# First loads on other queues, and unit 2's state half and block around the first feed-forward groups

## The chip, the cores and the metric

The kernel runs on one core of a Trainium2 chip. Its engines run side by side, each with its own queue of instructions, and wait for each other by semaphores: PE (TensorE, matmuls; its weight loads are listed as PEld), DVE (VectorE), ACT (ScalarE), POOL (GpSimd) and SP (SyncE, which here only starts transfers). SP, ACT and POOL can all start DMA transfers. The profile has one row for the transfers that POOL issues (software queue) and other rows for those of SP and ACT (hardware queues).

The metric is device time in microseconds (us), the median of several runs. The profile is that of one execution, and its times count from the first instruction.

## The reference: what is computed

A retention layer, and then a two-layer feed-forward network with a quick GELU.

```python
scores = scale * np.matmul(q, k.transpose(0, 1, 3, 2))      # q, k, v: 8 x 8 heads x 576 x 64
gamma = 1.0 - 2.0 ** (-5.0 - np.arange(H))
Dmat = np.where(rel >= 0, gamma[:, None, None] ** rel[None, :, :], 0.0)   # rel = i - j
ret = scores * Dmat[None, :, :, :]
x = np.matmul(ret, v)            # then tokens x (heads * 64): 4608 x 512
h = x @ w_in                     # 512 x 2048
g = h * (1.0 / (1.0 + np.exp(-1.702 * h)))
out = g @ w_out                  # 2048 x 512
```

Inputs and output are float32; the kernel's matmuls read bfloat16.

## The kernel before

**Units and chunks.** The 4608 tokens are cut into 36 units of 128 tokens, and four units make a chunk of 512. Since the decay gamma^(i-j) is a product of a factor of i and a factor of j, a unit needs no full score matrix: within each half of 64 tokens it uses masked scores, and what lies before comes from a running state (a sum of k times v over the earlier halves). V is multiplied by its factor on DVE (`scale_v`, L345, into `vp`) and the result by the factor of the query (`x_out`, L534, from PSUM times `gq` into `xT`).

**One unit of the beginning** (units 0 to 3) goes through these steps:

- `load(u)`: three transfers of 256 KB, K and Q (L226; units 1 and 2 load Q by L213) and V (L239). They are issued by POOL. K and Q are cast to bfloat16 on the way.
- `transpose_pe` (L361, L356): four or eight transposes on TensorE into PSUM, one set for K and one for Q, and `transpose_copy` on ACT (L374) or DVE (L377) into `kqT`.
- `scores(u)` (L497) on TensorE into psC and psD, `scores_out` (L506) on DVE: times the mask, into `pm`.
- `state_half(u, 0)`: `update`, eight matmuls k times vp into psK (L403), and a copy of psK on ACT into `kv` (L413).
- `block1(u)`: `inter` (L481, the state against Q), `values` (L519, pm against vp), in between `state_half(u, 1)`, and then the two `x_out` on DVE.

**Unit 0 is loaded apart.** `load_kq0` brings its K and its Q uncast into the output tiles osb1 and osb2, both issued by SP (L246), and `cast_kq0` casts them on DVE (L257). Its V comes as the first transfer on POOL's queue.

**The feed-forward part.** `up_group(c, f0, nf, lo, hi, bank)` multiplies nf of the 16 column blocks of w_in with the units lo to hi of chunk c (L570) and applies the GELU on ACT (L575); `up` is the same for a whole chunk (L556, GELU L561). `down` multiplies with w_out (L582), its result is copied (L592) and stored (L598). In the first chunk the up-groups are placed between the steps of the units as soon as x of two units is there.

**What sets the order.** The order of each engine's instructions is written out by hand in `lead_in` (units 0 to 7, chunk 0) and `steady` (the rest); the class `Program` finds the waits from the tiles that are read and written. Every engine takes its instructions strictly in that order. `lead_in` begins with the transfers: POOL makes three iotas and then issues V of unit 0, K, Q and V of units 1 and 2, two parts of w_in, unit 3, the rest of w_in, w_out, and units 4 to 11. `warm(n, bank, w)` puts n matmuls (L674) of w columns (512 if not told otherwise) on zeros in between; they give nothing that is used. ACT begins with the exponentials for the decay factors: eight `vfac` (L307), four `gq_first` (L315), four `g_powers` (L321), and then a small GELU (L687) that has the table of that function loaded early.

From unit 8 on K and Q are transposed by DMA, issued by SP (L391, `dma_transpose`). The first of these, unit 8, is placed after the load of V of unit 13, and the others of that group follow it in SP's queue:

```python
                    for u in range(8, 14):
                        dma_transpose(u, ["vn1"])
```

Here vn1 is the tile that holds V of unit 13 by then.

Of the kernel before, what the change touches and what calls it, by code (L numbers as in the profile page):

```python
# [11 lines left out]
B, H, S, DH = 8, 8, 576, 64  # L12
# [17 lines left out]
class Program:  # L30
# [10 lines left out]
    def op(self, eng, fn, reads=(), writes=(), dma=None, ndma=1, after_ops=()):  # L41
        o = Op()
        o.eng, o.fn, o.dma, o.signal, o.count = eng, fn, dma, False, None
        o.idx = len(self.streams[eng]) + 1
        deps = {}
        for k in reads:
            for d in self.writers.get(k, ()):
                deps[id(d)] = (d, True)
        for k in writes:
            for d in self.writers.get(k, ()) + self.readers.get(k, ()):  # L50
                deps.setdefault(id(d), (d, False))
        known = self.known[eng]
        need = []
        for d, raw in deps.values():
            if d.dma is None:
                if d.eng == eng and dma is None and (eng == "pe" or not raw):
                    continue
                agent, val = d.eng, d.idx
            else:
                agent, val = d.dma, d.dval  # L60
            need.append((agent, val, d))
        for d in after_ops:
            need.append((d.eng, d.idx, d))
        need.sort(key=lambda x: -x[1])
        waits = {}
        for agent, val, d in need:
            if known.get(agent, 0) >= val:
                continue
            if agent in waits and waits[agent][0] >= val:
                continue  # L70
            waits[agent] = (val, d)
        pruned = []
        for agent, (val, d) in waits.items():
            if any(
                a2 != agent and d2.known.get(agent, 0) >= val
                for a2, (_, d2) in waits.items()
            ):
                continue
            pruned.append(d)
        for agent, (val, d) in waits.items():  # L80
            d.signal = True
            known[agent] = max(known.get(agent, 0), val)
            for a2, v2 in d.known.items():
                if v2 > known.get(a2, 0):
                    known[a2] = v2
        o.waits = pruned
        o.known = dict(known)
        if dma is None:
            o.known[eng] = max(o.known.get(eng, 0), o.idx)
        else:  # L90
            self.dma_count[dma] = self.dma_count.get(dma, 0) + 16 * ndma
            o.dval = self.dma_count[dma]
            o.known[dma] = o.dval
        self.streams[eng].append(o)
        for k in writes:
            self.writers[k] = (o,)
            self.readers[k] = ()
        for k in reads:
            self.readers[k] = self.readers.get(k, ()) + (o,)
        return o  # L100
# [60 lines left out]
def bass_retnet_parallel__then__act_gelu_quick_kernel(  # L161
# [10 lines left out]
    with es:  # L172
# [35 lines left out]
        op = pr.op  # L208
# [25 lines left out]
        def load_v(u, after=(), eng="pool"):  # L234
            sl = u % NLD

            def f(e):
                return [
                    e.dma_start(vn[sl][p0 : p0 + n, :, :], v[b, :, s0 : s0 + n, :].rearrange("h p d -> p h d"))  # L239
                    for p0, n, b, s0 in unit_rows(u)  # L240
                ]
            op(eng, f, reads=after, writes=[f"vn{sl}"], dma=f"d_vn{sl}_{eng}", ndma=len(unit_rows(u)))

        def load_kq0(which):
            src = (k, q)[which]
            op("sp", lambda e: e.dma_start(  # L246
                osb[1 + which].ap().rearrange("p (h d) -> p h d", d=DH),
                src[0, :, 0:P, :].rearrange("h p d -> p h d")),
               writes=[f"osb{1 + which}_0"], dma=f"d_kq0f_{which}")
# [438 lines left out]
               reads=["warm"], writes=["gelu_table"])  # L688

        def lead_in():  # L690
            load_kq0(0)
            load_kq0(1)
            iota_small()
            iota_large()
            load_v(0)
            load(1)
            load(2)
            load_win(0, 2)
            load_win(2, 2)
            load(3)  # L700
            load_win(4, 2)
            load_win(6, 2)
            load_win(8, 4)
            load_win(12, 4)
            for i in range(4):
                load_wout(i)
            for u in range(4, NPE + 4):
                load(u)
            op("dve", lambda e: e.memset(gT[1][:, 0, :], 0.0), writes=["warm"])
            warm_quads(NQUAD)  # L710
            warm(44, "A", 64)
            setup_dve()
            setup_dve2()
            setup_vfac()
            for a in range(4):
                gq_first(a)
            g_powers()
            gelu_table()
            cast_kq0(0, "dve")
            transpose_pe(0, 0, "E")  # L720
            transpose_copy(0, 0, "E", "dve")
            cast_kq0(1, "dve")
            warm(4)
            transpose_pe(0, 1, "B")
            transpose_copy(0, 1, "B", "dve")
            scale_v(0)
            warm(2)
            scores(0)
            scores_out(0, 1, 0)
            scores_out(0, 1, 1)  # L730
            warm(1, "A", 256)
            state_half(0, 0)
            transpose_pe(1, 0, "E")
            transpose_copy(1, 0, "E", "act")
            transpose_pe(1, 1, "B")
            transpose_copy(1, 1, "B", "act")
            scale_v(1)
            block1(0)
            warm(1, "A", 256)
            scores(1)  # L740
            scores_out(1, 1, 0)
            scores_out(1, 1, 1)
            gq_next(1)
            warm(1)
            state_half(1, 0)
            transpose_pe(2, 0, "E")
            transpose_copy(2, 0, "E", "act")
            warm(1)
            block1(1)
            transpose_pe(2, 1, "B")  # L750
            transpose_copy(2, 1, "B", "act")
            warm(2)
            scores(2)
            scale_v(2)
            scores_out(2, 1, 0)
            scores_out(2, 1, 1)
            up_group(0, 0, 2, 0, 2, "A")
            state_half(2, 0)
            up_group(0, 2, 2, 0, 2, "B")
            gq_next(2)  # L760
            block1(2)
            transpose_pe(3, 0, "E")
            transpose_copy(3, 0, "E", "dve")
            transpose_pe(3, 1, "D")
            transpose_copy(3, 1, "D", "act")
            up_group(0, 0, 4, 2, 3, "A")
            scale_v(3)
            scores(3)
            scores_out(3, 1, 0)
            scores_out(3, 1, 1)  # L770
            gq_next(3)
            warm(1, "E", 256)
            state_half(3, 0)
            up_group(0, 4, 2, 0, 2, "B")
            block1(3)
            up_group(0, 4, 2, 2, 3, "A")
            up_group(0, 6, 2, 0, 2, "B")
            up_group(0, 0, 4, 3, 4, "C")
            up_group(0, 4, 2, 3, 4, "A")
            up_group(0, 6, 2, 2, 4, "B")  # L780
            gq_next(4)
            gq_next(5)
            for f in range(8, NF):
                up(0, f)
            def ahead45():
                ahead(2)
                for u in (4, 5):
                    state_sum(u, 0)
                    state_sum(u, 1)
                state_cast(4, 6)  # L790
                scores_out(4, 2, 0)
                scores_out(4, 2, 1)

            work = {
                (1, 3): lambda: (scale_v(4), transposes(4, "E", "D", "dve")),
                (2, 0): lambda: (transposes(5, "E", "D", "dve"), scale_v(5)),
                (2, 1): ahead45,
                (3, 1): lambda: block(2, lambda: None),
                (3, 2): lambda: (transposes(6, "C", "D", "dve"), scale_v(6)),
                (3, 3): lambda: (transposes(7, "E", "K", "dve"), scale_v(7)),  # L800
            }
            for r, s in [(i % 2, i // 2) for i in range(8)] + [(i // 4, i % 4) for i in range(8, NF)]:
                down(0, r, s, "AB"[r % 2])
                if (r, s) in work:
                    work[r, s]()
                if s == 3:
                    finish_unit(0, r, "AB"[r % 2])
# [130 lines left out]
```

## Time and profile before

| what | value |
| --- | --- |
| median of the runs | 295.63 us (295.49, 295.63, 296.52) |
| span of the profiled execution | 293.4 us |
| what lies around the span, against the median | 2.2 us |
| TensorE busy | 287.7 us, 98% |
| ScalarE, GpSimd, VectorE busy | 133.7, 110.2, 99.7 us |
| moved by DMA | 40.63 MB, mean 139 GB/s |
| share of POOL's queue, of SP's (of 16 engines' span) | 68.0%, 24.8% |
| mean granted TensorE clock | 0.999 |

The profile lists for an instruction its start, its duration, its engine and line, and what it writes and reads (out<-in, numbers of tiles left out). In brackets stands the time for which the engine had been idle and what ended that. For a DMA the duration is that of issuing it; the time to landing is told apart. The chain of waits goes back from the last instruction to whatever released it. The profiled execution's time outside the span is not recorded; it is taken as the difference to the median of the runs.

In the first microseconds the transfers land as follows, from the start of their issue (from the rows of the single lines): K of unit 0 after 3.1 us, Q of unit 0 after 3.5, V of unit 0 after 6.5, K, Q and V of unit 1 after 5.7, 5.4 and 5.5. DMA engines moved 279 GB/s from 2.2 to 4.4 us, 178 and 186 in the two microseconds after that, and 204 from 20 to 24 us.

### The profile page before, as it was taken

To read this page: it belongs to the slowest core of one execution; us is meant where nothing else is said; L and a number is where in the kernel's file an instruction comes from. 1 tells how busy PE (TensorE), PEld (TensorE's weight loads), DVE (VectorE), ACT (ScalarE), POOL (GpSimd) and SP (SyncE) were. 2 spreads that over 40 slices of the span, in tenths; PEclk is the share of its full clock that TensorE was granted. 3 is DMA by queue.
4 is the path that set the end of the run, shared out by engine and by line. 5 is a ranking of instruction groups with operands and counts; after the bars stand their busy time and mean duration, and the time that the engine had idled before them with its cause. 6 is when DMAs were issued, how large, how long until landed. Compare 5 with 4: busy or idle time off the path is not lost.

```text
span 293.4 us, 8059 instructions
## 1 busy us (share of the span) xinstructions
PE 287.7 (98%) x3650; PEld 141.2 (48%) x3650; DVE 99.7 (34%) x202; ACT 133.7 (46%) x235; POOL 110.2 (38%) x141
## 2 busy tenths in 40 slices
PE   8899999999999999999999999999999999999996
PEld 6575456775533553345334533454344434443344
DVE  5861056615650652054404360237013700410000
ACT  7466234661366135712672256324642365216611
POOL 9999798000960590292049103910170000000000
PEclk9999999999999999999999999999999999999999
DMA  9999999998999899799479935992692050111022
GB/s 172 175 211 206 209 231 249 235 120 213 125 236 115 98 230 227 93 161 200 133 106 153 188 108 113 178 182 80 137 142 71 20 131 2 38 72 38 0 65 78
DMA packets 116786, 40.63 MB, mean 139 GB/s; under 512 B 104080, under 2 KB 109968, under 8 KB 116752
## 3 DMA queue, kind: packets, MB, share of 16 engines
q0 software_dynamic: 79712, 22.82, 68.0%
q1 hardware_dynamic: 36896, 17.24, 24.8%
q8 instruction: 28, 0.46, 0.7%
q10 hardware_dynamic: 144, 0.07, 0.1%
q14 instruction: 6, 0.05, 0.0%
HBM read 36.70 MB, written 9.44 MB: 157 GB/s over the span
## 4 chain that ended last, share of the span: by engine, by line
PE 96%; DMA 2%; DVE 1%; issue 0%; ACT 0%; POOL 0%; POOLq 0%
PE psA L582 22%; PE psB L582 21%; PE psA L556 18%; PE psB L556 18%; PE psB L570 4%; PE psA L570 3%; DMA vn<-in_v_dram 2%; PE psX L481 2%; PE psC L497 1%; PE psY L519 1%; PE psX L519 1%; PE psK L426 1%; PE psD L497 1%; PE psE L426 1%; PE psK L403 1%; PE psE L361 0%
## 5 line engine op out<-in xcount | busy, mean ns | idle before, releaser
L226 POOL DMA_DIRECT2D kqn<-in_k_dram x39 | 35.1, 910 | 106.9 <-DMA kqT<-kqn 104.9
L582 PE MATMUL psA<-w_out_sb,gT 128*128 128x512 bf16 (+1 forms) x304 | 69.4, 371 | 0.3 <-issue 0.3
L582 PE MATMUL psB<-w_out_sb,gT 128*128 128x512 bf16 (+1 forms) x288 | 65.4, 376 | 0.0
L556 PE MATMUL psA<-xT,w_in_sb 128*128 128x512 bf16 x240 | 61.6, 379 | 0.0
L556 PE MATMUL psB<-xT,w_in_sb 128*128 128x512 bf16 x240 | 61.6, 379 | 0.0
L544 DVE TENSOR_TENSOR xT<-psX,gq 128x512 bf16<-128x512 f32 x16 | 11.1, 691 | 109.3 <-PE psX L519 109.3
L450 ACT ACTIVATE kv<-stm 128x1024 bf16<-128x1024 f32 (+1 forms) x18 | 15.6, 866 | 68.7 <-DVE stm L441 68.7
L582 PEld LDWEIGHTS psB<-w_out_sb,gT 128*128 128x128 bf16 x288 | 27.8, 98 | 32.5 <-ACT gT L561 0.3
L561 ACT ACTIVATE gT<-psB 128x512 bf16<-128x512 f32 x60 | 35.8, 597 | 15.8 <-PE psB L556 15.7
L561 ACT ACTIVATE gT<-psA 128x512 bf16<-128x512 f32 x60 | 35.8, 597 | 15.6 <-PE psA L556 15.6
L582 PEld LDWEIGHTS psA<-w_out_sb,gT 128*128 128x128 bf16 x304 | 27.2, 98 | 31.9 <-ACT gT L561 2.5
L239 POOL DMA_DIRECT2D vn<-in_v_dram x40 | 37.1, 942 | 0.1
L556 PEld LDWEIGHTS psA<-xT,w_in_sb 128*128 128x128 bf16 x240 | 19.2, 97 | 32.7 <-ACT gT L561 16.6
L556 PEld LDWEIGHTS psB<-xT,w_in_sb 128*128 128x128 bf16 x240 | 18.8, 97 | 33.0 <-ACT gT L561 16.4
L345 DVE TENSOR_TENSOR vp<-vn,vfac 128x512 bf16<-128x512 f32 x36 | 23.4, 684 | 30.8 <-DMA vn<-in_v_dram 30.8
L226 POOL DMA_DIRECT2D kqn<-in_q_dram x37 | 33.4, 917 | 0.6 <-issue 0.6
L592 ACT ACTIVATE osb<-psB 128x512 f32<-128x512 f32 (+1 forms) x18 | 10.6, 590 | 22.7 <-PE psB L582 22.5
L592 ACT ACTIVATE osb<-psA 128x512 f32<-128x512 f32 x18 | 10.5, 584 | 15.3 <-PE psA L582 15.3
L506 DVE TENSOR_TENSOR pm<-psC,mask 128x512 bf16<-128x512 f32 (+1 forms) x20 | 12.6, 628 | 8.7 <-PE psD L497 8.7
L506 DVE TENSOR_TENSOR pm<-psD,mask 128x512 bf16<-128x512 f32 (+1 forms) x20 | 12.5, 626 | 0.0
L570 PE MATMUL psB<-xT,w_in_sb 128*128 128x256 bf16 x96 | 12.5, 273 | 0.0
L441 DVE TENSOR_TENSOR stm<-psE,stm 128x256 f32<-128x256 f32 x28 | 11.9, 424 | 1.2
(86 smaller groups left out, 257.3 us busy)
## 6 DMA issues: line engine op xcount, KB each, us to landing
vn<-in_v_dram POOLq DMA_DIRECT2D x32, 256.0 KB, 5.6
out_dram<-osb SPq DMA_DIRECT2D x31, 256.0 KB, 2.6
kqn<-in_k_dram POOLq DMA_DIRECT2D x31, 128.0 KB, 5.5
kqn<-in_q_dram POOLq DMA_DIRECT2D x31, 128.0 KB, 5.7
w_out_sb<-in_moe_w_out_dram POOLq DMA_DIRECT2D x4, 512.0 KB, 13.3
w_in_sb<-in_moe_w_in_dram POOLq DMA_DIRECT2D x8, 128.0 KB, 5.0
w_in_sb<-in_moe_w_in_dram POOLq DMA_DIRECT2D x4, 256.0 KB, 7.2
vn<-in_v_dram POOLq DMA_DIRECT2D x8, 128.0 KB, 7.0
```

The lines of the kernel that those rows point to most:

```text
L226: e.dma_start(kqn[sl][p0 : p0 + n, which, :, :], src[b, :, s0 : s0 + n, :].rearrange("h p d -> p h d"),)
L239: e.dma_start(vn[sl][p0 : p0 + n, :, :], v[b, :, s0 : s0 + n, :].rearrange("h p d -> p h d"))
L345: op(eng, lambda e: e.tensor_tensor(vp[u % NVP].ap(), vn[sl].ap(), vfac[:, ty, :, None].to_broadcast([P, H, DH]), ALU.mult), reads=[f"vn{s ...
L441: op("dve", lambda e: e.tensor_tensor(dst, src, prev, ALU.add), reads=[KB[a], f"stm{(i - 1) % 8}"], writes=[f"stm{i % 8}"])
L450: op("act", lambda e: e.activation(kv[:, i0 % NKV : i0 % NKV + n, :, :], stm[:, i0 % 8 : i0 % 8 + n, :, :], AF.Copy), reads=[f"stm{(i0 + i ...
L506: op("dve", lambda e: e.tensor_tensor(pm[(u0 // 2) % 2][hh][:, c0:c1].rearrange("p (a i) -> p a i", i=64), ps32(SB[hh])[:, c0:c1].rearrang ...
L544: op("dve", lambda e: e.tensor_tensor(xT[ch % 2][:, slice(hh, 4, 2), P * jj : P * jj + 2 * P].rearrange("p g (u t) -> p u g t", u=2), ps32 ...
L556: op("pe", lambda e, a=a: e.matmul(bank[b][:, n0:n1], w_in_sb[:, a, P * f : P * f + P], xT[c % 2][:, a, n0:n1], start=(a == 0), stop=(a == ...
L561: op("act", lambda e: e.activation(gT[c % 2][:, f, n0:n1], bank[b][:, n0:n1], AF.Gelu_apprx_sigmoid), reads=[b], writes=[f"g{c % 2}_{f}_{j ...
L570: op("pe", lambda e, a=a, f=f, i=i: e.matmul(bank[b][:, n * i : n * i + n], w_in_sb[:, a, P * f : P * f + P], xT[c % 2][:, a, P * lo : P * ...
L582: op("pe", lambda e, f=f: e.matmul(bank[b][:, 0 : n1 - n0], gT[c % 2][:, f, P * r : P * r + P], w_out_sb[:, f, n0:n1], start=(f == 0), sto ...
L592: op("act", lambda e: e.activation(dst, src, AF.Copy), reads=[b], writes=[f"osb{i}_{n0}"])
```

## The change

Four edits in `lead_in`, and a parameter for `load_kq0`:

- K of unit 0 stays on SP; Q of unit 0 is issued by ACT, as its first instruction; V of unit 0 is issued by SP, behind K, and is no longer on POOL's queue.
- The cast of Q of unit 0 goes from DVE to ACT, between the second and the third of the four `gq_first`.
- Warming matmuls: one instead of four ahead of Q's transposes, three of 512 columns instead of one of 256 ahead of unit 0's first state half, and none instead of one of 256 ahead of unit 3's.
- `state_half(2, 0)` stands ahead of the first feed-forward group instead of behind it, and `gq_next(2)` and `block1(2)` stand ahead of the second group instead of behind it.

```diff
-        def load_kq0(which):
+        def load_kq0(which, eng):
             src = (k, q)[which]
-            op("sp", lambda e: e.dma_start(
+            op(eng, lambda e: e.dma_start(
...
         def lead_in():
-            load_kq0(0)
-            load_kq0(1)
+            load_kq0(0, "sp")
+            load_kq0(1, "act")
+            load_v(0, eng="sp")
             iota_small()
             iota_large()
-            load_v(0)
             load(1)
...
             setup_vfac()
-            for a in range(4):
-                gq_first(a)
+            gq_first(0)
+            gq_first(1)
+            cast_kq0(1, "act")
+            gq_first(2)
+            gq_first(3)
             g_powers()
             gelu_table()
             cast_kq0(0, "dve")
             transpose_pe(0, 0, "E")
             transpose_copy(0, 0, "E", "dve")
-            cast_kq0(1, "dve")
-            warm(4)
+            warm(1)
             transpose_pe(0, 1, "B")
...
             scores_out(0, 1, 1)
-            warm(1, "A", 256)
+            warm(3)
             state_half(0, 0)
...
             scores_out(2, 1, 1)
+            state_half(2, 0)
             up_group(0, 0, 2, 0, 2, "A")
-            state_half(2, 0)
-            up_group(0, 2, 2, 0, 2, "B")
             gq_next(2)
             block1(2)
+            up_group(0, 2, 2, 0, 2, "B")
             transpose_pe(3, 0, "E")
...
             gq_next(3)
-            warm(1, "E", 256)
             state_half(3, 0)
```

## The prediction

> **What bounds the kernel now.** I read the page's share of busy time first, then the chain of waits over the first 40 us, then the order of time of the first 10 us, and last the landings of single transfers.
>
> ```profile
> span 293.4 us, 8059 instructions
> PE 287.7 (98%) x3650; PEld 141.2 (48%) x3650; DVE 99.7 (34%) x202; ACT 133.7 (46%) x235; POOL 110.2 (38%) x141
> ```
>
> TensorE is 98% busy and is the chain that ended last for 96% of the span. From 24.7 us on its matmuls follow one another, so nothing there is for this change to win; all it can do is let the dense part start earlier. A microsecond won in the first 25 us is worth a microsecond at the end, if no transfer is late afterwards. The chain (start, us, what) shows what the start waits for:
>
> ```profile
> 1.42 6.49 DMA vn<-in_v_dram
> ...
> 16.83 0.77 DVE xT L534 x2
> ...
> 18.95 0.21 PE psE L674
> ```
>
> The first V (unit 0) is issued by POOL at 1.42 and lands at 7.91; only then can DVE scale it and TensorE make the first state half, at 8.68. At 16.83 TensorE waits for the two x_out products of unit 2, although two transposes lie beside them; the groups after it start at 17.64. The last line is a warming matmul that computes nothing. In the order of time (start, us, engine, line, tile; in brackets the idle time before it):
>
> ```profile
> 0.73 0.46 SPq L246 DMA_DIRECT2D osb<-in_k_dram  x1
> 1.25 0.57 SPq L246 DMA_DIRECT2D osb<-in_q_dram  x1
> ...
> 1.42 1.03 POOL L239 DMA_DIRECT2D vn<-in_v_dram  x1
> ...
> 3.46 1.63 ACT L315 ACTIVATE gq<-iota_c,lnsc,lng 128x128 f32<-128x128 f32 x4
> ...
> 4.87 1.69 PE L674 MATMUL psA<-gT 128*128 128x512 bf16 x4
> ...
> 5.46 0.60 DVE L257 CAST kqn<-osb 128x512 bf16<-128x512 f32 x1
> ...
> 6.62 0.59 PE L674 MATMUL psA<-gT 128*128 128x512 bf16 x2
> ...
> 7.93 0.69 DVE L345 TENSOR_TENSOR vp<-vn,vfac 128x512 bf16<-128x512 f32 x1 [0.69 <-DMA vn<-in_v_dram]
> ...
> 9.54 0.69 DVE L345 TENSOR_TENSOR vp<-vn,vfac 128x512 bf16<-128x512 f32 x1 [0.26 <-DMA vn<-in_v_dram]
> ```
>
> Four warming matmuls at 4.87 take 1.69 us, two at 6.62 take 0.59: the array runs at half speed until about 6.2 us. The last two rows say that V is late twice: unit 0 by 0.69, unit 1 by 0.26. Unit 1's transfers stand right behind the first V on POOL's queue.
>
> One place far from the change matters as well. SyncE's transpose of unit 9 starts at 64.8 and lands 2.7 later, at 67.55; TensorE reads it for unit 9's scores at 67.60. SyncE's queue had waited for V of unit 13, which POOL issued at 50.1 and which landed 12.6 later (the waits of SyncE's queue; us in total, times, longest):
>
> ```profile
> SPq L116 <- DMA vn<-in_v_dram: 12.3, 1, 12.3
> ```
>
> So at 67.6 us TensorE and the stream of transfers meet within 0.05 us. TensorE can be earlier there only by as much as POOL's stream is earlier.
>
> **The change part by part.** Times are in the profiled execution, whose span is 293.4; the median of the runs shown, 295.63, lies 2.2 above it, which is what stands around a span and is left as it is.
>
> *K, Q and V of unit 0.* K keeps its place on SP (0.73). Q's issue (0.57) moves to ScalarE, ahead of its first table load (1.28 from 0.73). That load then ends near 2.6; the first exponential waited until 2.67 for DVE anyway, so the issue costs nothing; without that cover it would cost its 0.57. V takes Q's place on SP at 1.25. K alone needed 3.06 from issue to landing, Q behind it 3.55. K now shares the engines with Q: it lands between 3.80 (as now) and 4.80 (when both had landed before); I take the middle, 4.3, and 4.5 for Q. V is the third 256 KB; the first two moved at 279 GB/s between 2.2 and 4.4 us (the table of stretches), which makes 0.9 us more than Q: 5.4 to 6.0.
>
> *Q's cast* leaves DVE (0.60) for ScalarE, after two of the four gq exponentials (3.46 + 0.82 = 4.28): an ACTIVATE of 128x512, 0.60 by the kqT rows, from 4.5 to 5.1. The other exponentials, gpow (0.47), gelu's table load (1.28) and gelu (0.20) follow 0.8 to 1.2 later and end at 7.8 to 8.1 instead of 6.97; ScalarE was idle 2.05 us before its state copy at 9.03, and that hides it; without this cover the cast's 0.60 would be lost. A copy under the exponential's table does not occur in this trace: at worst it adds two table loads, 2 x 1.28, at best none; under gelu's table copies run without one, the nearest row, so I take none.
>
> *Three warming matmuls fewer ahead of Q's transposes* (4 to 1). At half speed they held TensorE from 4.87 to 6.40, past the end of Q's cast (6.06). Now: K cast 4.3 to 4.8, K transposes to 5.5, one warming matmul to 5.9, Q transposes 6.3, DVE's copy 6.7, scale_v(0) until 7.4, three warming matmuls (0.65 at full speed, +0.9 at half) instead of one beside it, first state half at 7.5 to 7.8 instead of 8.68: 0.9 to 1.2 earlier.
>
> *What is late next.* With V off POOL's queue every POOL issue moves up by that issue, 1.03. Unit 1's K, Q and V needed 5.7, 5.4 and 5.5 from issue to landing, so V of unit 1 would land at 2.99 + 5.5 = 8.5 instead of 9.52. At the other end the stream's first transfer is slow (V needed 6.5, 1.0 more than its followers) and now has V on SP beside it: 9.2. Nearest are its own rows after the first, so 8.5. ScalarE's chain (state copy at 8.1, kqT copies until 9.5) gives unit 1's scores at 9.5 instead of 10.49. Lead: 1.0, ends 0.35 and 1.05.
>
> *Unit 2's state half and block.* No instruction is added. Ahead of the first feed-forward group the state half meets vp of unit 2, ready at 13.98, when scores(2) end at 13.9: 0.1 lost. Its state copy on ScalarE now precedes the group's gelu (0.38) and is hidden under that group (0.98). The second group, 0.98, now lies over x_out (0.77) and removes TensorE's wait before 17.64 (who waited for whom, us in total):
>
> ```profile
> PE psA L570 <- DVE xT L534: 0.3, 1, 0.3
> ```
>
> Behind it ScalarE gets gelu of that group (0.60) before unit 3's kqT copy, which then ends at 18.1 in before's time, ahead of the scores. With the removed warming matmul (0.21) the part gives 0.31 - 0.10 + 0.21 = 0.4; ends 0.1 (the wait comes back behind gelu) and 0.5.
>
> *Sum on TensorE:* 1.0 + 0.4 = 1.4 earlier at 24.7 us.
>
> *Sum on POOL's stream.* At unit 9 it may take 0.05 plus what the stream gained. The stream loses one issue, 1.03, or 256 KB at the 204 GB/s that it moves from 20 to 24 us, 1.25. V on SP may take back its own transfer, 256 KB at 279 GB/s or 0.92, which leaves 0.33. Of these ends I go by the rows: from 2.4 to 14 us landings lie 4.6 to 6.2 us behind their issues without growing, so the stream there follows its issues, 1.03. Unit 5's V and Q land about 0.4 before their use at 40 us, so up to there 1.03 + 0.4 = 1.4 passes. Of the 1.4 on TensorE, then, 1.05 stays: 295.63 - 1.05 = 294.6.
>
> Two rules speak against this. The Trainium skill (DMA: Bandwidth & Descriptors, Issuing engines are not separate DMA queues) says that transfers from all issuing engines run on the same 16 engines and interleave, so that spreading issuers saves only issue time. Read strictly, V on SP takes its 0.92 from the same engines and the sum is 295.3 instead of 294.6; no row of this trace shows SP's and ScalarE's queues side by side. The Trainium skill (TensorE: Matmul & The Clock Gate, Part 1) says that full speed comes only after a free-running window of some 3.4 us filled with matmuls, and its Part 4 that transposes don't count as such. The rows agree on a step at 6.2; by the rule thinner warming could miss the window, and an estimate with the next one, at 9.6, gives about 295.1.
>
> **The rivals.** *A, nothing ends the gain:* the stream gains by its bytes, 1.25 + 0.05 = 1.3, or more, and TensorE's sum stands at up to its upper end, 1.05 + 0.5 = 1.55: 294.1 to 294.3. For it: 256 KB less at 204 GB/s. Against: the lag behind the issues does not grow before 14 us.
>
> *B, the next transfers eat it:* POOL's first transfer stays slow, so V of unit 1 lands at 9.2, lead 0.35, or the stream gains only 0.33: 0.3 to 0.7, 295.1. For it: 6.49 against 5.5 for the first transfer. Against: its slowness coincides with K and Q on SP, done at 4.80.
>
> *C, slower: the array stays at half speed longer,* since 4.87 to 6.2 us holds one warming matmul and K's transposes instead of four. Until the first state half it costs five warming matmuls x 0.21 = 1.05, of which 0.6 lies under the waits: 0.45 net, 295.1. From 13.9 on each feed-forward group of 0.98 costs 0.98 more: one makes 296.0, slower than before, three 298.0. So it decides from 14 us. Against: TensorE has work for more than half of the time from 4.9 to 9.6.
>
> *D, the change does less than it says:* K waits for Q so long (4.80) that unit 0 is no earlier than ScalarE's later table load permits; that ends in B's numbers and is counted there.
>
> **How the numbers follow.** Forecast (gain 0.7 to 1.3, that is 294.3 to 294.9): 0.39. A: 0.25. B and D (gain 0 to 0.7): 0.22. C: 0.14, of which 0.12 above 297.1. About 0.5% (1.48 us) is what a measurement of this kernel can tell from no change: faster is most of A, whose times lie at that edge, with the spread of the runs, 0.2; slower is C, 0.12; the rest 0.68. Runs of one kernel lie 1.0 apart here (295.49 to 296.52), so I widen A's end by 0.4, to 293.7, and let the upper end take in B and C's near part: 296.7.
>
> **What would show it.** Right: V's scaling near 6.7 without a DMA wait, the first state half before 7.9, V of unit 1 at 8.5, no wait before unit 2's four-group matmuls, dense work from 23.3, and a gap of some 0.3 before unit 9's scores where TensorE waits for SyncE's transpose. Wrong: warming matmuls at 0.43 each after 7 us, unit 1's V at 9 or later, an extra table load, or dense work and unit 9's scores shifted by the same amount.

## The result and the profile after

The changed kernel takes 294.14 us (median of 6, 293.58 to 294.68) against 295.5 (median of 6, 295.08 to 296.52): 1.36 us or 0.46% less, ratio 0.995, 95% interval [0.9933, 0.9968]. Measured again in another series the ratio was 0.9959 [0.9946, 0.9973]. The forecast was 294.6.

The profiled execution of the changed kernel is one of its slower ones (294.68). Its page begins:

```profile
span 292.9 us, 8023 instructions
PE 283.2 (97%) x3617; PEld 141.1 (48%) x3648; DVE 98.8 (34%) x201; ACT 134.3 (46%) x236; POOL 109.3 (37%) x140
```

The lines of its order of time that answer to those of before (start, us, engine, line, tile, idle time before):

```profile
0.74 0.48 ACTq L246 DMA_DIRECT2D osb<-in_q_dram  x1
...
1.25 0.57 SPq L239 DMA_DIRECT2D vn<-in_v_dram  x1
...
4.85 0.63 ACT L254 ACTIVATE kqn<-osb 128x512 bf16<-128x512 f32 x1 [0.54 <-DMA osb<-in_q_dram]
...
7.06 0.68 DVE L345 TENSOR_TENSOR vp<-vn,vfac 128x512 bf16<-128x512 f32 x1
...
8.77 0.69 DVE L345 TENSOR_TENSOR vp<-vn,vfac 128x512 bf16<-128x512 f32 x1 [0.36 <-DMA vn<-in_v_dram]
```

DVE no longer waits for unit 0's V, which landed at 5.76; unit 1's V still ends a wait, at 8.77 instead of 9.54. TensorE's wait before unit 2's four-group matmuls is gone: they start at 16.80 instead of 17.64, and the dense part about 1.2 earlier. But of this lead nothing is left at 67.6 us. Who waited for whom between 60 and 75 us:

```profile
PEld psC L497 <- DMA kqT<-kqn: 1.7, 2, 1.0
...
PE psC L497 <- DMA kqT<-kqn: 1.1, 2, 0.8
```

TensorE stands 1.1 us before the scores of units 8 and 9, waiting for SyncE's transposes. The chain of waits now runs along POOL's issues to V of unit 13, and from there over a transpose to TensorE (start, us, what):

```profile
48.59 12.66 DMA vn<-in_v_dram
...
62.79 4.78 DMA kqT<-kqn
```

V of unit 13 lands at 61.25 instead of 62.63. The transpose of unit 9 needed 4.8 from issue to landing instead of 2.7, so in this execution it landed at 67.57, as late as before. In the 14 traces of this study it is before's 2.7 that is rare: eleven need 3.4 to 4.8, and only before, V only and no warming need 2.7. What the execution still gained, 0.5 in the span, came from elsewhere, between 203 and 233 us: there TensorE in before's profile had lost 0.3, at 221 us, where it waited for nothing that the profile shows. One execution of each kernel is thus not enough to say where 1.36 us come from; the runs below say more.

### The profile page after: what moved, and what is told of

Read it like the earlier page. It is cut to its first block, busy times and chain, and to the rows that moved or that the text cites. A ratio compares the mean times of both kernels' runs of the same rounds, so it can differ in the third digit from the quotient of the medians.

```text
span 292.9 us, 8023 instructions
## 1 busy us (share of the span) xinstructions
PE 283.2 (97%) x3617; PEld 141.1 (48%) x3648; DVE 98.8 (34%) x201; ACT 134.3 (46%) x236; POOL 109.3 (37%) x140
## 4 chain that ended last, share of the span: by engine, by line
PE 75%; POOL 16%; DMA 6%; issue 2%; SPq 0%; DVE 0%; POOLq 0%
PE psB L582 19%; PE psA L582 18%; PE psA L556 17%; PE psB L556 16%; POOL kqn L226 8%; DMA vn<-in_v_dram 4%; POOL vn L239 4%; POOL w_in_sb L261 3%; DMA kqT<-kqn 2%; PE psX L481 1%; POOL w_out_sb L268 1%; PE psC L497 1%; PE psX L519 1%; PE psK L426 1%; PE psE L426 1%
## 5 line engine op out<-in xcount | busy, mean ns | idle before, releaser
L582 PE MATMUL psA<-w_out_sb,gT 128*128 128x512 bf16 (+1 forms) x287 | 65.7, 370 | 2.4 <-issue 2.2
L582 PE MATMUL psB<-w_out_sb,gT 128*128 128x512 bf16 (+1 forms) x285 | 64.7, 376 | 0.5 <-issue 0.5
L556 PE MATMUL psA<-xT,w_in_sb 128*128 128x512 bf16 x239 | 61.4, 379 | 0.1
L544 DVE TENSOR_TENSOR xT<-psX,gq 128x512 bf16<-128x512 f32 x16 | 11.1, 692 | 113.8 <-PE psX L519 113.8
L239 POOL DMA_DIRECT2D vn<-in_v_dram x39 | 35.6, 925 | 0.0
L556 PEld LDWEIGHTS psA<-xT,w_in_sb 128*128 128x128 bf16 x240 | 19.2, 97 | 32.7 <-ACT gT L561 16.6
```

Of the source, the lines that this page charges most:

```text
L544: op("dve", lambda e: e.tensor_tensor(xT[ch % 2][:, slice(hh, 4, 2), P * jj : P * jj + 2 * P].rearrange("p g (u t) -> p u g t", u=2), ps32 ...
L556: op("pe", lambda e, a=a: e.matmul(bank[b][:, n0:n1], w_in_sb[:, a, P * f : P * f + P], xT[c % 2][:, a, n0:n1], start=(a == 0), stop=(a == ...
L582: op("pe", lambda e, f=f: e.matmul(bank[b][:, 0 : n1 - n0], gT[c % 2][:, f, P * r : P * r + P], w_out_sb[:, f, n0:n1], start=(f == 0), sto ...
```

## The experiments

Every run has one profiled execution beside its timed ones. The table puts four moments of these side by side: the start of unit 1's scores, the landing of the second part of w_in, the start of the matmuls into psC that end the mixed stage, and the landing of V of unit 13, which ends POOL's first stream. Each ratio is against before's runs of the same series. Their medians are 295.51 for order only, the late reads and loads only, 295.66 for Q only, V only, V again and two V, and 295.68 for the others from after, again on.

| kernel | unit 1's scores | w_in, part 2 | psC | V of unit 13 | median | ratio to before, 95% interval |
| --- | --- | --- | --- | --- | --- | --- |
| before | 10.49 | 13.00 | 22.30 | 62.63 | 295.5 | |
| order only | 10.04 | 13.10 | 22.59 | 62.97 | 295.68 | 1.0005 [0.9985, 1.0025] |
| before, late read | 9.58 | 13.66 | 22.88 | 62.53 | 295.29 | 0.9999 [0.9984, 1.0014] |
| Q only | 9.84 | 14.05 | 22.69 | 63.60 | 295.99 | 1.0015 [1.0, 1.003] |
| V only | 11.77 | 13.28 | 25.78 | 61.80 | 297.12 | 1.0044 [1.0013, 1.0075] |
| V again on POOL | 10.86 | 13.12 | 21.91 | 62.70 | 295.05 | 0.9984 [0.9968, 1.0001] |
| two V on SP | 10.38 | 12.61 | 21.86 | 61.89 | 295.56 | 1.0003 [0.999, 1.0016] |
| after | 10.06 | 12.23 | 21.11 | 61.25 | 294.14 | 0.995 [0.9933, 0.9968] |
| after, again | 9.61 | 12.34 | 20.67 | 61.20 | 294.08 | 0.9959 [0.9946, 0.9973] |
| loads only | 9.55 | 12.31 | 21.35 | 61.73 | 293.97 | 0.9949 [0.993, 0.9969] |
| after, late read | 9.52 | 12.20 | 20.58 | 61.07 | 293.8 | 0.9948 [0.9928, 0.9968] |
| after, one warming | 9.63 | 12.15 | 20.71 | 61.16 | 294.27 | 0.9959 [0.9944, 0.9974] |
| after, no warming | 9.69 | 12.38 | 22.86 | 61.66 | 295.14 | 0.999 [0.9975, 1.0005] |
| after, earlier transposes | 9.56 | 12.22 | 20.61 | 61.68 | 293.89 | 0.995 [0.9933, 0.9967] |

Two columns are worth comparing before any single run. The start of unit 1's scores does not decide the time: "before, late read" starts them at 9.58 and is no faster than before, "after" starts them at 10.06 and is. Part of its spread is the moment at which the array reaches full speed. Warming matmuls of 512 columns start 0.43 us apart ahead of that moment and 0.21 behind it; the moment lies near 6.9 us in the first trace of the changed kernel, before 5.9 in the second, and near 8.7 in "V again on POOL".

The landing of V of unit 13 goes with the time: with V of unit 0 on POOL it lies at 62.5 to 63.6 (mean of five 62.9), with V on SP behind K, and no second V there, at 61.1 to 61.7 (mean of seven 61.4). The difference, 1.5, is about what the time moved. Unit 9's transpose, which follows it, lands at 68.4 and 66.9 (means of the same five, and of six: without "earlier transposes"). An early landing alone is not enough. V only (61.80), two V on SP (61.89) and no warming (61.66) have it and win little or nothing; in their traces TensorE itself comes to unit 9 later than the transpose.

### The loads alone

```diff
 (from the changed kernel)
-            state_half(2, 0)
             up_group(0, 0, 2, 0, 2, "A")
-            gq_next(2)
-            block1(2)
+            state_half(2, 0)
             up_group(0, 2, 2, 0, 2, "B")
+            gq_next(2)
+            block1(2)
...
             gq_next(3)
+            warm(1, "E", 256)
```

> The loads, the cast and the warming matmuls of unit 0 as changed; unit 2's order and the warming matmul ahead of unit 3's state half as before. My reading of the changed kernel's trace (theory G, a gate at unit 9: what TensorE wins passes only as far as POOL's stream of transfers wins too): TensorE is 0.43 earlier from unit 1's scores on (10.06 against 10.49), POOL's stream 1.4 earlier, so nothing is gated: 0.43 less than before, about 295.05, dense matmuls at 24.25. Rival L (the loads carry the whole gain): 294.1.

Measured: 293.97, ratio 0.9949 [0.993, 0.9969]. The loads carry the whole gain; my figure, 295.05, was wrong. It came from the two profiles, in which TensorE was only 0.43 earlier at unit 1; the table shows that this distance is the chance of two executions. The trace of this kernel has no wait for unit 9's transpose: it lands at 67.06, and the scores that read it start at 67.10.

### The order of unit 2 alone

```diff
 (from the kernel before)
+            state_half(2, 0)
             up_group(0, 0, 2, 0, 2, "A")
-            state_half(2, 0)
-            up_group(0, 2, 2, 0, 2, "B")
             gq_next(2)
             block1(2)
+            up_group(0, 2, 2, 0, 2, "B")
...
-            warm(1, "E", 256)
             state_half(3, 0)
```

> Unit 2's order and the removed warming matmul ahead of unit 3's state half alone; the loads as before. Theory G: TensorE is 0.75 earlier at 24.7 (1.19 less 0.44), but V of unit 13 lands no earlier (62.6), so TensorE waits about 0.75 before unit 9's scores and the time is before's: 295.4 to 295.6. Rival P (what TensorE wins at 24.7 passes to the end): 294.75.

Measured: 295.68, ratio 1.0005 [0.9985, 1.0025]: no gain, the time that theory G named, but not by its way: there is no wait at unit 9. TensorE's waits from 8 to 72 us:

```profile
PE psA L570 <- issue: 1.1, 1, 1.1
PE psE L361 <- DMA kqn<-in_k_dram: 0.6, 1, 0.6
PE psD L361 <- DMA kqn<-in_q_dram: 0.2, 1, 0.2
```

The time was lost much earlier than I had expected, at K and Q of unit 3 (16.5 and 17.5 us), which come on POOL's queue too. The wait for "issue" is taken up at the end.

### A later read of units 8 and 9, in after and in before

```diff
 (after; the same edit in before)
                         if c == 1 and (r, s) == (0, 2):
-                            ahead(4)
-                            ahead_out(4)
+                            for u in (8, 9):
+                                state_both(u)
+                            for u in (8, 9):
+                                state_sum(u, 0)
+                                state_sum(u, 1)
+                            state_cast(8, 10)
+                        if c == 1 and (r, s) == (0, 3):
+                            scores(8)
+                            scores(9)
+                            scores_out(8, 2, 0)
+                            scores_out(8, 2, 1)
```

> The changed kernel, and the scores of units 8 and 9 in the second feed-forward stage one group of four matmuls later (0.86), behind the state sums. Theory G: the wait for unit 9's transpose, 1.1 in the changed kernel's trace, falls below 0.3, the lead of 1.2 at 24.7 reaches the end: 293.9 or less in the median and a smaller spread. Rival S (the wait is of that one execution, the median doesn't have it): 294.15, as without this edit.

> The kernel before with the scores of units 8 and 9 one group later. Theory G: before meets the transfer within 0.05, so 0.05 to win: 295.4 to 295.5. Rival (before too waits there in most executions, and its trace is a lucky one): 0.3 or more less, 295.2 or below.

Measured: 293.8 (0.9948 [0.9928, 0.9968]) and 295.29 (0.9999 [0.9984, 1.0014]). The wait at unit 9 is gone in both traces. In before this is worth nothing, as theory G said. In after the median is in the range of theory G, 0.3 under that of the first series, which the intervals can't tell from nothing (ratios 0.9948 and 0.995); its trace stands 1.2 us near 22 us for "issue" instead. So it is not shown that the wait at unit 9, 0.8 to 1.1 in the changed kernel, costs its length. The trace of the second kernel shows why before can't use a better start. Here V of unit 0 landed at 5.58, on POOL's queue, and DVE scaled it at 7.03, as early as after the change:

```profile
7.03 0.68 DVE L345 TENSOR_TENSOR vp<-vn,vfac 128x512 bf16<-128x512 f32 x1
```

And TensorE gave the time back at the first feed-forward groups (waits from 8 to 72 us):

```profile
PE psA L570 <- DMA w_in_sb<-in_moe_w_in_dram: 0.7, 1, 0.7
PE psB L570 <- DMA w_in_sb<-in_moe_w_in_dram: 0.7, 1, 0.7
PE psA L570 <- DVE xT L534: 0.3, 1, 0.3
```

So POOL's stream gates TensorE at several places, at whichever comes first: w_in at 13 to 15 us, K and Q of unit 3 at 16 to 17, unit 5 at 40, unit 9's transpose at 67.

### V alone and Q alone

V of unit 0 on SP behind K and Q, the rest as before; and the loads part with V left on POOL:

```diff
 (V only, from before)
             load_kq0(1)
+            load_v(0, eng="sp")
             iota_small()
             iota_large()
-            load_v(0)
 (Q only, from the loads alone)
             load_kq0(1, "act")
-            load_v(0, eng="sp")
             iota_small()
             iota_large()
+            load_v(0)
```

> From before: V of unit 0 on SP behind K and Q, and nothing else of the change. Theory S (all of the gain is that POOL's stream of transfers starts one issue, 1.03, earlier; what TensorE wins at its start is given back where it waits for that stream): 1.0 to 1.4 less than before, 294.1 to 294.5. Rival U (the earlier Q, its cast on ScalarE and the fewer warming matmuls bring a good part): 0.5 or less, 295.0 or more.

> From before: Q of unit 0 on ScalarE's queue, its cast on ScalarE and the warming matmuls of unit 0 as changed; V of unit 0 stays on POOL, unit 2's order as before. Theory S: before's time, 295.3 to 295.7. Rival U: 0.5 or more less, 295.0 or below.

Measured: 297.12 (1.0044 [1.0013, 1.0075]) and 295.99 (1.0015 [1.0, 1.003]). Q alone gives nothing, as theory S has it. It differs from the loads alone in one thing, the queue that brings V of unit 0: 295.99 with POOL, 293.97 with SP (ratios 1.0015 and 0.9949). That is the plainest measure of what V's place is worth once Q has left SP. With Q alone TensorE waits for the stream at w_in and at unit 9:

```profile
PE psA L570 <- DMA w_in_sb<-in_moe_w_in_dram: 0.8, 1, 0.8
PE psC L497 <- DMA kqT<-kqn: 0.7, 1, 0.7
```

V alone was against theory S: it made the kernel slower. Third on SP, V landed at 9.1 instead of 5.76 (DVE's order of time):

```profile
9.13 0.69 DVE L345 TENSOR_TENSOR vp<-vn,vfac 128x512 bf16<-128x512 f32 x1 [2.37 <-DMA vn<-in_v_dram]
```

The packets in the trace say why. In the changed kernel SP and ACT feed the engines together, the last of V's packets start at about 5.4, and the first of POOL's start only at 4.9: they hardly meet. Where V stands third, its packets run from 4.5 to 8.5 us, at 140 or fewer in a quarter of a microsecond instead of 280, among those of unit 1's K and Q from POOL, which start at 3.9. TensorE then stood for 2.5 us, and lost its clock after that:

```profile
PE psK L403 <- DVE vp L345: 2.5, 1, 2.5
```

Busy time by stretches (PE, PEld, DVE, ACT, POOL, each with its instructions; then the granted clock, the DMA share and GB/s):

```profile
4.00:11.00 7.00, 4.09 (x83) 2.45 (x83) 3.62 (x8) 3.73 (x11) 7.00 (x11) 1.00 1.50 217
11.00:18.00 7.00, 6.19 (x133) 4.08 (x120) 4.61 (x12) 2.88 (x7) 7.00 (x12) 0.51 1.64 205
18.00:25.00 7.00, 6.69 (x165) 5.18 (x164) 3.69 (x10) 4.20 (x9) 7.00 (x10) 1.00 1.25 206
```

From 11.2 to 18.0 the array ran at half speed. In 7 of 12 executions the mean clock was 0.994 or less, and these took 296.5 to 299.2; the other five, at 1.0, took 295.05 to 295.55, 0.6 to 0.1 under before's median: even these are not the 294.1 to 294.5 of theory S. Half speed is what rival C feared, here in a kernel that has half of the change. That the wait took the clock is argued from the order of the two; no run varied its length.

### One transfer more on POOL, and one less

```diff
 (V again on POOL, from after)
             iota_large()
+            op("pool", lambda e: e.dma_start(
+                osb[3].ap().rearrange("p (h d) -> p h d", d=DH),
+                v[0, :, 0:P, :].rearrange("h p d -> p h d")),
+               writes=["osb3_0"], dma="d_again")
             load(1)
 (two V on SP, from after)
             load_v(0, eng="sp")
+            load_v(1, eng="sp")
             iota_small()
             iota_large()
-            load(1)
+            load_kq(1, 0)
+            load_kq(1, 1)
```

> The changed kernel, and V of unit 0 loaded a second time, first on POOL's queue, into an output tile that nobody reads by then (one transfer more than needed). Theory S: the stream is where it was before the change, and so is the time: 295.2 to 295.6, with waits of TensorE for w_in, K or Q of unit 3 or the transpose of unit 9. Rival U: 294.2 to 294.5.

> The changed kernel, and V of unit 1 on SP too, behind V of unit 0: POOL's stream starts another issue, 0.92, earlier. Theory S: earlier again, but now TensorE's own lead (1.2 at 24.7) is the smaller: 0.2 to 0.5 less than the changed kernel, 293.6 to 293.9. Rival (SP's transfers now hold up K and Q of unit 1 on the same 16 engines, or the gain is used up): 294.1 or more.

Measured: 295.05 (0.9984 [0.9968, 1.0001]) and 295.56 (1.0003 [0.999, 1.0016]). A transfer that nobody needs, put where V had stood, takes back more than half of the gain (0.9984 instead of 0.995), with the changed kernel's code otherwise in place; V of unit 13 lands at 62.70 again. TensorE waits for the stream at units 9 and 5:

```profile
PE psC L497 <- DMA kqT<-kqn: 0.3, 1, 0.3
...
PE psD L361 <- DMA kqn<-in_q_dram: 0.2, 1, 0.2
```

So one more transfer at the head of POOL's queue costs time even when unit 0's V comes early. It does not take back all, 0.15 under the range that I had set, and it does not say whether the issue or the 256 KB counts, for it adds both.

A second V on SP takes the gain away. POOL's issues are 0.9 earlier again, but V of unit 13 lands at 61.89, not earlier than with one V, and Q of unit 1 at 9.19 instead of 8.01. In its trace TensorE is the late one: it comes to unit 9 after the transpose. Two of its waits:

```profile
PE psA L570 <- issue: 1.1, 1, 1.1
PE psB L356 <- DMA kqn<-in_q_dram: 0.7, 1, 0.7
```

### The start of TensorE, its clock and the last gate

The changed kernel again; with one warming matmul in place of three ahead of the first state half; with none between K's transposes and unit 2's scores; and with SyncE's transposes waiting for V of unit 12.

```diff
 (one warming)
-            warm(3)
+            warm(1)
             state_half(0, 0)
 (no warming: warm(1), warm(2), warm(3), warm(1, "A", 256), warm(1), warm(1), warm(2) taken out)
 (earlier transposes)
-                        dma_transpose(u, ["vn1"])
+                        dma_transpose(u, ["vn0"])
```

> The changed kernel once more, beside the others of this call. Theory S (the gain is POOL's stream starting an issue earlier, with V in the time before that stream's first packets; TensorE's own lead beyond it is given back at unit 9): 294.0 to 294.4, about 0.005 of before's time less, as with the loads alone. Rival (unit 2's order adds to the loads): 0.3 or more below the loads alone, 293.6 or less.

> The changed kernel with one warming matmul instead of three ahead of unit 0's state half, which in its trace stood behind them (vp ready at 7.74, state half at 8.24). TensorE wins up to 0.5 at its start. Theory S: nothing of it arrives, 294.0 to 294.4. Rival U (the start of TensorE sets the end): 293.6 to 293.8. Rival C (the array falls back to half speed): 295 or more in some executions, at a mean clock under 0.995.

> The changed kernel without any warming matmul from K's transposes of unit 0 to unit 2's scores. Rival C as the price of a cold array: the clock comes later or is taken away as where V stood third on SP (6.8 us at half speed): 1.5 to 3.5 more, 295.6 to 297.7, mean clock 0.988. If the array stays at full speed all the same: 293.7 to 294.4.

> The changed kernel, but SyncE's transposes from unit 8 on wait for V of unit 12 instead of V of unit 13, 2.3 earlier. Theory G (unit 9's transpose is the last gate): it lands 1 to 2 earlier, TensorE no longer waits there, 293.4 to 293.8. Rival (the transposes now share the engines with the last loads and are as late as before, or the gain is used up elsewhere): 294.0 or more.

Measured: 294.08, 294.27, 295.14 and 293.89, ratios 0.9959 [0.9946, 0.9973], 0.9959 [0.9944, 0.9974], 0.999 [0.9975, 1.0005] and 0.995 [0.9933, 0.9967].

The second execution of the changed kernel waits 0.8 for unit 9's transpose, which takes 4.3 from issue to landing:

```profile
PE psC L497 <- DMA kqT<-kqn: 0.8, 1, 0.8
```

One warming matmul instead of three wins nothing, and all 12 executions have a mean clock of 1.0. Without warming matmuls the array fell to half speed in most executions (mean clock 0.983 in 9 of 12):

```profile
8.00:18.00 10.00, 9.31 (x200) 6.92 (x199) 6.18 (x14) 5.31 (x12) 10.00 (x16) 0.50 1.56 214
```

With ten microseconds at half speed the psC matmuls come 2.2 later than in the changed kernel's second trace (22.86 against 20.67), and the median is 1.06 higher (295.14 against 294.08 in the same series). Some of the 2.2 is time that TensorE would have stood at unit 9 anyway, 0.8 in the changed kernel's trace; here it comes there 2 us after the transpose. But half speed is not the whole 1.06. The nine executions that lost the clock have a median of 295.28, and the three at 1.0 took 294.73 to 294.95: within this kernel the clock costs 0.4, and the larger part is lost with the clock whole. No trace shows these three, so where they lose it stays open.

With earlier transposes the wait at unit 9 is gone, and a small new one appears at unit 5, near 39 us:

```profile
PE psE L361 <- DVE kqT L377: 0.3, 1, 0.3
...
PE psD L361 <- DMA kqn<-in_q_dram: 0.2, 1, 0.2
```

The median, 293.89, lies between the two theories, 0.2 under that of the changed kernel in the same series, which the intervals can't tell from nothing. As with the late read, taking the wait at unit 9 away wins little: other waits take its place. No kernel of this study is clearly faster than the changed one.

## Why the prediction was right, and where it was not

**The time lay in the range, and the stream counts: right.** The forecast took the smaller of what TensorE and what POOL's stream win. That the stream counts is shown by V's place (Q only against the loads alone), by the order alone and by the second V on POOL. That unit 9's transpose is the place where it counts is only in part shown. A wait there of some 0.3 was forecast; it was 1.1 (with unit 8) and 0.8 in the two traces of the changed kernel. The loads alone speak for it: they come to it just as it lands (67.10 against 67.06) and take the same time. Against it: where the wait was taken away, the medians fell by 0.3 and 0.2, which the intervals can't tell from nothing. The meeting within 0.05 that the forecast built on was luck of the trace: it rests on a transpose of 2.7, and eleven of 14 traces have 3.4 to 4.8.

**"Sum on POOL's stream" was mis-sized: 1.03, measured 1.5** (62.9 to 61.4 for V of unit 13). The bytes, 1.25, were the nearer end. I had gone by the issues, since landings lay an even distance behind them up to 14 us. (The 0.05 at unit 9 and 1.03 make 1.08, not 1.05.) Another part of what the forecast lacked lies in its base. In every run whose time and span are both on record the two are 1.8 apart, not 2.2, so before's profiled execution took about 295.15 (an estimate, 293.35 + 1.8), 0.35 under before's median.

**V on SP did take something back, at the head.** POOL's first packets start at 4.6 to 5.0 us in the nine traces with V second on SP, and at 3.7 to 4.0 in the other five. V of unit 2 lands at 11.1 to 11.3 in the seven traces with V on SP behind K and no second V, and at 11.2, 11.2, 11.4 and 12.1 with V on POOL: almost no gain so far. It shows from the first part of w_in on, at 10.7 to 11.1 instead of 11.6 to 12.0. Why it shows there first, and why it grows to 1.5, no run tells.

**The strict reading of the Trainium skill's rule** (DMA: Bandwidth & Descriptors, Issuing engines are not separate DMA queues) fits the head of the stream, and it fits V third on SP and two V on SP, where the transfers overlap: 9.1 instead of 5.76 for V itself, and no further gain of the stream. Its price for this change, 295.3, did not come: from w_in on the stream was ahead.

**"Lead: 1.0" on TensorE was wrong in kind.** V landing at 7.91 was the chance of the execution that I read: with V on POOL it landed at 5.42 and 5.58 in the traces of the order alone and of before with the late read. In such executions before starts as early as after does, and loses the time at w_in and at unit 3's K and Q instead. I had named only unit 5 and unit 9 as places where the stream gates. Unit 1's V at 9.52 was chance too: it landed at 8.60, 8.76 and 8.98 in the three other traces that have unit 0's V on POOL alone.

**Unit 2's order: 0.4 on TensorE forecast, worth nothing alone.** In the second trace of the changed kernel and in that of the loads alone, which start alike (9.61 and 9.55), it brings psC 0.68 earlier (20.67 against 21.35). The two kernels take the same time (0.9959 and 0.9949); in the trace of the first, TensorE stands 0.8 at unit 9.

**The small steps** held in the main: K landed at 4.33 (4.3 forecast), Q at 4.82 (4.5), V at 5.76 (5.4 to 6.0); Q's cast took 0.63 on ScalarE, with no further table load; unit 1's V landed at 8.75 (8.5). K's cast took 0.82 on DVE instead of 0.43, which I had not counted. V's scaling started at 7.06 and 6.65 in the two traces (6.7 forecast) and the first state half at 8.24 and 7.79 (7.5 to 7.8): the later ones are of the trace in which the array reached full speed near 6.9.

**The rivals.** A came by its number: 294.14 lies in its 294.1 to 294.3, and just outside the 294.3 to 294.9 that the forecast gave itself. Of its two terms the stream's gain did go beyond the bytes (1.5); that nothing ends TensorE's gain is not so, for TensorE waited at unit 9 in both traces. B's fear, the next transfers held up by V, came only in two V on SP and V only. C did not come here, where every execution had a mean clock of 0.999 or more, but one step away: V alone lost its clock in 7 of 12 executions, and these took 296.5 to 299.2, C's price for one group and more. Without warming matmuls lost clock cost 0.4, far less than the microsecond that I had reckoned for each group. The step to full speed near 9.6, from which the prediction estimated 295.1, was near 6.9 and before 5.9 in the changed kernel's two traces.

## What to carry to other kernels

Where one queue of transfers feeds a kernel for its first 60 us, a transfer taken off the head of that queue can be worth its share of the queue, here 1.5 us at the queue's end. It matters where it goes: second on SP, ahead of POOL's first packets, it paid; third on SP, or with one more behind it, it fell among the other transfers and did not. The two moves needed each other: Q had to leave SP for V to be early enough there, and each alone gave nothing or worse. A chain of waits from one execution shows what was late in that execution: look at a second one before a term is built on a single late transfer, and list every place where the same stream is waited for, not the first and the last.

## What the runs showed of the hardware that was not expected

- **After a gap of 2.5 us the clock was at half for 6.8 us.** With V third on SP TensorE stood from 7.35 to 9.87 and was at half speed from 11.2 to 18.0, while it worked. Without warming matmuls it was at half speed from 7.8 to 18.0 although no gap was longer than 0.7: here small matmuls with short waits between them did not hold the clock.
- **The granted clock does not show the slow start.** Before's warming matmuls from 4.87 us on start 0.43 apart and those at 6.62 and 6.83 start 0.21 apart, but the granted clock reads 1.00 over the whole stretch from 4.4 to 7.2 us. In V again on POOL they start 0.42 apart up to 8.7 us, again at 1.00. The half speed of those first microseconds is read from the matmuls alone.
- **TensorE sometimes stands 1.1 to 1.2 us near 22 to 24 us for nothing that the profile names.** This was in four traces (order only, after with the late read, two V on SP, one warming). For the second:

```profile
PEld psA L570 <- issue: 1.4, 1, 1.4
```

  A 16 KB packet of the instruction queue starts 1 to 1.3 us ahead of the gap's beginning in each of them, at 20.9 to 22.6; in the traces of the changed kernel without the gap it starts at 19.2 and 19.8. Measured from the start of the psC matmuls, these packets start between 0.02 us ahead of it and 0.3 behind in the four traces with the gap, and 1.2 to 2.3 us ahead of it in the ten without. That TensorE waits for its own instructions there is argued, not shown.
- **SyncE's transposes are slow where an instruction packet falls between them.** In the first trace of the changed kernel one of 1.88 us starts at 62.7; the transpose of unit 8 needs 5.1 us to landing and that of unit 9 takes 2.9 to issue instead of 1.24. In all eleven traces with 3.4 or more for unit 9's transpose, such a packet starts between unit 8's issue and unit 9's landing. V only, with 2.7, has none there; before, with 2.7, has one at 63.2 that comes ahead of unit 9's issue, and no warming, with 2.7, one only 0.4 ahead of unit 9's landing. Whether the one causes the other was not tried.
